# An mLSTM cell with a dropless mixture of experts: keys and queries transposed in fp32 from zero-padded rows, row scaling on GpSimd, clears and weight loads moved

## The chip, the core and the metric

The kernel runs on one core of one Trainium2 chip. The metric is the device time of one execution in microseconds, from the core's first to its last instruction; the number given for a kernel is the median of its timed executions. Engine names in the profile: PE is TensorE (matmul), PEld its weight loads, DVE VectorE, ACT ScalarE, POOL GpSimd, SP SyncE. A `q` after a name (SPq, POOLq) is that engine's sequencer or DMA queue.

## The reference

Two stages. First an mLSTM cell over a sequence, with batch 4, 8 heads, 768 positions and head width 40. It is written as a recurrence:

```python
for t in range(S):
    m_new  = max(f_gate[t] + m, i_gate[t])
    f_stab = exp(f_gate[t] + m - m_new);  i_stab = exp(i_gate[t] - m_new);  m = m_new
    C = f_stab * C + i_stab * outer(v[t], k[t])        # 40 x 40 for each batch and head
    n = f_stab * n + i_stab * k[t]
    y[t] = sigmoid(o_gate[t]) * (C @ q[t]) / max(abs(n . q[t]), 1)
```

Then the rows y (3072 rows of 8 heads x 40 = 320 columns) go through a mixture of 8 experts: `logits = x @ w_gate`, each row goes to the expert with the largest logit, `relu(x @ w1[e]) @ w2[e]` with 1024 hidden columns, times the softmax weight of the chosen expert.

## The kernel before

The recurrence is computed in chunks of 128 positions: 24 steps, 6 chunks for each of 4 batches. Each step s is a pipeline of small functions, run for different s in one pass of the loop. Inside a chunk there is a masked product of queries and keys (`scores`, `attend`); the state from earlier chunks is `C` (`states`). Heads go in pairs (PR = 4 pairs), because two heads of 40 fit on 128 partitions.

```python
DP = 64; DQ = 2 * D; D1 = D + 1                       # D = 40
NKQ = 3
kqb = [consts.tile([128, 2, H, DP], BF16) for i in range(NKQ)]     # bf16 k and q, heads padded to 64
v1  = [consts.tile([128, H, D1], F32) for i in range(NV)]

def first_consts():
    make_identity(nc, ident[:]);  nc.vector.tensor_copy(ident_b[:], ident[:])
    nc.vector.memset(zeros_s[:], 0.0)
    for t in kqb: nc.vector.memset(t[:, :, :, D:], 0.0)
    for t in v1:  nc.vector.memset(t[:, :, D:], 1.0)
    nc.vector.memset(zrow[:], 0.0)
    nc.vector.memset(w1_all[:64, DB - 1], 0.0)        # L91: 64 x 4096 words

def gates():                                          # scans over the sequence, exp, transposes to G_T, m_T
    nc.vector.tensor_tensor_scan(F_sb[:], f_sb[:], zeros_s[:], 0.0, op0=ALU.add, op1=ALU.add)   # L200
    ...

def load(s):                                          # k, q, v, o of one chunk, 160 KB each, on SP
    ...
def casts(s):                                         # L226, L227
    nc.gpsimd.tensor_copy(d["kqb"][:, 0, :, :D], d["k"][:])
    nc.gpsimd.tensor_copy(d["kqb"][:, 1, :, :D], d["q"][:])

def transposes(s):
    for i in range(2):
        for j in range(PR):                           # 8 bf16 transposes, L249
            nc.tensor.transpose(tkq[:, i, j, :], <two heads of kqb>, ident_b[:])
    nc.scalar.copy(d["kqT"][:], tkq[:])               # L253
    if s % NB > 0:
        for j in range(PR):                           # 4 fp32 transposes of q, L257
            nc.tensor.transpose(tq[:, j, :], <two heads of q>, ident[:])
        nc.scalar.copy(d["qT"][:], tq[:])             # L261

def scores(s):                                        # L269, L270; masked to dA (DVE, L274),
    ...                                               # and dB (ACT L276, then POOL affine_select L277)
def states(s):                                        # L289: hp = qT . C;  L297: dC += k . vA;  L303: C = dC * bdm
    ...
def attend(s):                                        # L309: hp += dA or dB . vAb
    ...
def rows(s):
    nc.vector.scalar_tensor_tensor(x3d, in0=th, scalar=1.0, in1=hp[:, :, :D], op0=ALU.add, op1=ALU.mult)   # L321
    <den = max(|2 n.q|, m_T): two operations, L323, L324>
    nc.vector.reciprocal(den[:], den[:])
    nc.vector.tensor_tensor(x3d, x3d, den[:].unsqueeze(2).to_broadcast([128, H, D]), op=ALU.mult)          # L326

def xtrans(s):                                        # three fp32 transposes of x (L333), copied by ACT (L335)
    ...
# logits (L351), choose (L361 to L373), gate, rank (L398), place (L409, L411): the router, for two steps at a time
def keep_rows(t): ...                                 # ACT L416: x_all[:, t] = x * gate weight, bf16
def send(t):      ...                                 # POOL L423: scatter of the rows to x_sorted, by slots
def clear(e):                                         # ACT's DMA queue, L429: zeros to the rows of expert e in x_sorted
    nc.scalar.dma_start(xs[e * NS : e * NS + CAP, :]..., zrow[:])
def weights(e0, n):                                   # POOL's DMA queue, fp32 to bf16: L170 (w1, three parts), L171 (w2)
    ...

for i in range(5): load(i)
for s in range(-3, NT + 3):
    do(load, s + 6 if s >= -1 else -1)
    do(scores, s + 1); do(transposes, s + 2); do(casts, s + 3)
    if s == -3: masks()
    if s == -2: gates(); router()
    do(values, s + 2)                                 # L235: vA = v * G (DVE); L237: vAb = bf16 of vA (POOL)
    if -1 <= s < 3: clear(2 * s + 2); clear(2 * s + 3)
    if not odd and P >= 0: gate(P)
    do(states, s); do(xtrans, s - 1)
    do(ogate, s + 2)                                  # L242: th = tanh(o / 2) (ACT)
    do(attend, s)
    if odd and s >= 3: logits((s - 3) // 2, s)
    if not odd and P >= 0: rank(P, s)
    do(keep_rows, s - 4); do(rows, s)
    if odd and s >= 3: choose((s - 3) // 2)
    if not odd and P >= 0: place(P)
    do(send, s - 5)
    if s == 20: weights(0, 3)                         # w1 and w2 of the first three experts
```

(The tail of the loop, where the last rows are sent, is left out.) After the loop the experts follow: `receive` loads each expert's rows from x_sorted (L538), `turn` transposes them (L569), `layer1` (L578) and `layer2` (L591) multiply, and the results are scattered to the output (L597). A tile of a pool that is full is given out again only when its last reader is done, and PE, ACT, DVE and POOL each take their instructions in the order of the program.

Of the kernel before, what the change touches and what calls it, by code (L numbers as in the profile page):

```python
# [8 lines left out]
F32 = mybir.dt.float32  # L9
BF16 = mybir.dt.bfloat16  # L10
# [4 lines left out]
ALU = mybir.AluOpType  # L15
# [4 lines left out]
def kernel(  # L20
# [13 lines left out]
    nc = tc.nc  # L34
    B, H, S, D = q.shape
    BH = B * H
# [6 lines left out]
    NT = N // 128  # L43
    PR = H // 2
    DP = 64
    DQ = 2 * D
    D1 = D + 1
    LG = H * D1
    RW = Dm + 2
# [22 lines left out]
    ident_b = consts.tile([128, 128], BF16)  # L72
    cmask = consts.tile([128, 128], F32)
    bdm = consts.tile([DQ, PR, 2, D1], F32)
    zeros_s = consts.tile([BH, S], F32)
    NKQ = 3
    kqb = [consts.tile([128, 2, H, DP], BF16, name=f"kqb{i}") for i in range(NKQ)]
    v1 = [consts.tile([128, H, D1], F32, name=f"v1_{i}") for i in range(NV)]
    zrow = consts.tile([128, NJ * RW], BF16)

    def first_consts():
        make_identity(nc, ident[:])
        nc.vector.tensor_copy(ident_b[:], ident[:])
        nc.vector.memset(zeros_s[:], 0.0)

        for t in kqb:
            nc.vector.memset(t[:, :, :, D:], 0.0)
        for t in v1:
            nc.vector.memset(t[:, :, D:], 1.0)
        nc.vector.memset(zrow[:], 0.0)  # L90
        nc.vector.memset(w1_all[:64, DB - 1], 0.0)  # L91

    def masks():

        nc.gpsimd.memset(cmask[:], 1.0)
        nc.gpsimd.affine_select(
            cmask[:], cmask[:], compare_op=ALU.is_ge, fill=0.0,
            base=0, pattern=[[1, 128]], channel_multiplier=-1,
        )

        nc.gpsimd.memset(bdm[:], 1.0)
        nc.gpsimd.affine_select(
            bdm[:], bdm[:], compare_op=ALU.is_ge, fill=0.0,
            base=0, pattern=[[0, PR], [-D, 2], [0, D1]], channel_multiplier=1,
        )
        nc.gpsimd.affine_select(
            bdm[:], bdm[:], compare_op=ALU.is_ge, fill=0.0,
            base=D - 1, pattern=[[0, PR], [D, 2], [0, D1]], channel_multiplier=-1,
        )


# [52 lines left out]
    slots = rte.tile([128, NT], I32)  # L164
    tot = rte.tile([128, E], F32)

    def weights(e0, n):
        e = slice(e0, e0 + n)
        for db, (d0, dsz) in enumerate(dch):
            nc.gpsimd.dma_start(w1_all[128 - dsz :, db, e, :], moe_w1[e, d0 : d0 + dsz, :].rearrange("e p f -> p e f"))  # L170
        nc.gpsimd.dma_start(  # L171
            w2_all[:, e].rearrange("p e a d -> p (e a) d"), moe_w2[e].rearrange("e (a p) d -> p (e a) d", p=128),
        )

    def apart(ins, group):
        ins = getattr(ins, "ins", ins)
# [8 lines left out]

    one_order = ExitStack()
    one_order.enter_context(tc.manual_schedule())
    with tc.tile_pool(name="gates", bufs=1) as gate_pool, \
         tc.tile_pool(name="ld", bufs=6) as ld, \
         tc.tile_pool(name="prep", bufs=3) as prep, \  # L190
         tc.tile_pool(name="chk", bufs=2) as chk, \
         tc.tile_pool(name="ps1", bufs=1, space=PSUM) as ps1, \
         tc.tile_pool(name="ps2", bufs=2, space=PSUM) as ps2:
        st = {}
        f_sb = gate_pool.tile([BH, S], F32)
        i_sb = gate_pool.tile([BH, S], F32)

        def gates():
            F_sb = gate_pool.tile([BH, S], F32)
            nc.vector.tensor_tensor_scan(F_sb[:], f_sb[:], zeros_s[:], 0.0, op0=ALU.add, op1=ALU.add)  # L200
            g_sb = gate_pool.tile([BH, S], F32)
            nc.vector.tensor_sub(g_sb[:], i_sb[:], F_sb[:])
            M_sb = gate_pool.tile([BH, S], F32)
            nc.vector.tensor_tensor_scan(M_sb[:], g_sb[:], g_sb[:], -1e30, op0=ALU.max, op1=ALU.max)
            negc = gate_pool.tile([BH, 1], F32)
            nc.vector.tensor_scalar_mul(negc[:], M_sb[:, S - 1 : S], -1.0)
            for src, e_sb, dst, mul in ((g_sb, F_sb, G_T, 1.0), (M_sb, f_sb, m_T, 2.0)):
                nc.scalar.activation(e_sb[:], src[:], AF.Exp, bias=negc[:], scale=1.0)
                tpg = ps1.tile([128, NB, BH], F32, name="tpg", tag="xt")
                for c in range(NB):  # L210
                    nc.tensor.transpose(tpg[:, c, :], e_sb[:, c * 128 : (c + 1) * 128], ident[:BH, :BH])
                nc.vector.tensor_scalar_mul(
                    dst[:].rearrange("p b c h -> p c b h"), tpg[:].rearrange("p c (b h) -> p c b h", b=B), mul,
                )

        def load(s):
            b, c = s // NB, s % NB
            d = st[s] = {}
            for n, src in (("k", k), ("q", q), ("v", v), ("o", o_gate)):
                d[n] = v1[s % NV] if n == "v" else ld.tile([128, H, D], F32, name=n + "_sb")  # L220
                nc.sync.dma_start(d[n][:, :, :D], src[b, :, c * 128 : (c + 1) * 128, :].rearrange("h p d -> p h d"))

        def casts(s):
            d = st[s]
            d["kqb"] = kqb[s % NKQ]
            nc.gpsimd.tensor_copy(d["kqb"][:, 0, :, :D], d["k"][:])  # L226
            nc.gpsimd.tensor_copy(d["kqb"][:, 1, :, :D], d["q"][:])  # L227

        def values(s):

# [12 lines left out]

        def transposes(s):
            d = st[s]
            tkq = ps1.tile([128, 2, PR, 128], BF16, name="tkq")
            for i in range(2):
                for j in range(PR):
                    nc.tensor.transpose(  # L249
                        tkq[:, i, j, :], d["kqb"][:, i, 2 * j : 2 * j + 2, :].rearrange("p h d -> p (h d)"), ident_b[:],  # L250
                    )
            d["kqT"] = prep.tile([128, 2, PR, 128], BF16, name="kqT")
            nc.scalar.copy(d["kqT"][:], tkq[:])  # L253
            if s % NB > 0:
                tq = ps1.tile([DQ, PR, 128], F32, name="tq")
                for j in range(PR):
                    nc.tensor.transpose(  # L257
                        tq[:, j, :], d["q"][:, 2 * j : 2 * j + 2, :].rearrange("p h d -> p (h d)"), ident[:],
                    )
                d["qT"] = prep.tile([DQ, PR, 128], F32, name="qT")  # L260
                nc.scalar.copy(d["qT"][:], tq[:])  # L261

        def scores(s):
            d = st[s]
            kqT = d["kqT"]
            sA = ps1.tile([128, PR, 128], F32, name="sA")
            sB = ps1.tile([128, PR, 128], F32, name="sB")
            for j in range(PR):
                nc.tensor.matmul(sA[:, j, :], lhsT=kqT[0:D, 0, j, :], rhs=kqT[0:D, 1, j, :], start=True, stop=True)  # L269
                nc.tensor.matmul(  # L270
                    sB[:, j, :], lhsT=kqT[64 : 64 + D, 0, j, :], rhs=kqT[64 : 64 + D, 1, j, :], start=True, stop=True,
                )
            d["dA"] = chk.tile([128, PR, 128], BF16, name="dA")
            nc.vector.tensor_tensor(d["dA"][:], sA[:], cmask[:, None, :].to_broadcast([128, PR, 128]), op=ALU.mult)  # L274
            d["dB"] = chk.tile([128, PR, 128], BF16, name="dB")
            nc.scalar.copy(d["dB"][:], sB[:])  # L276
            nc.gpsimd.affine_select(  # L277
                d["dB"][:], d["dB"][:], compare_op=ALU.is_ge, fill=0.0,
                base=0, pattern=[[0, PR], [1, 128]], channel_multiplier=-1,
            )  # L280

        def states(s):
# [10 lines left out]
            if c + 1 < NB:  # L293
                if c == 0:
                    st["dC"] = ps1.tile([DQ, PR, 2, D1], F32, name="dC")
                for j in range(PR):
                    nc.tensor.matmul(  # L297
                        st["dC"][:, j], lhsT=d["k"][:, 2 * j : 2 * j + 2, :].rearrange("p h d -> p (h d)"),
                        rhs=d["vA"][:, 2 * j : 2 * j + 2, :],
                        start=(c == 0 and j == 0), stop=True, skip_group_check=True,  # L300
                    )
# [12 lines left out]
        def rows(s):  # L314
# [8 lines left out]
            nc.vector.scalar_tensor_tensor(den[:], in0=hp[:, :, D], scalar=-2.0, in1=m_T[:, b, c, :], op0=ALU.mult, op1=ALU.max)  # L323
            nc.vector.scalar_tensor_tensor(den[:], in0=hp[:, :, D], scalar=2.0, in1=den[:], op0=ALU.mult, op1=ALU.max)  # L324
            nc.vector.reciprocal(den[:], den[:])
            nc.vector.tensor_tensor(x3d, x3d, den[:].unsqueeze(2).to_broadcast([128, H, D]), op=ALU.mult)  # L326

        def xtrans(s):

# [101 lines left out]
        def do(f, i, *a):  # L431
            if 0 <= i < NT:
                f(i, *a)
# [5 lines left out]
            nc.scalar.dma_start(wg_sb[128 - dsz :, db, :], moe_w_gate[d0 : d0 + dsz, :])  # L439
        first_consts()  # L440
        for i in range(5):
            load(i)
        for s in range(-3, NT + 3):
            tail = s >= NT
            P, odd = (s - 4) // 2, s % 2
            do(load, s + 6 if s >= -1 else -1)
            do(scores, s + 1)
            do(transposes, s + 2)
            do(casts, s + 3)
            if s == -3:  # L450
                masks()
            if s == -2:
                gates()
                router()
            do(values, s + 2)
            if -1 <= s < 3:
                clear(2 * s + 2)
                clear(2 * s + 3)
            if not odd and P >= 0:
                gate(P)  # L460
            do(states, s)
            do(xtrans, s - 1)
            do(ogate, s + 2)
            do(attend, s)
# [19 lines left out]
                send(s - 3)  # L484
            late_consts(s + 1)
            if s == 20:
                weights(0, 3)

    xg = [x_all[:, e * NJ : (e + 1) * NJ, :] for e in range(E)]
    sm_pool = ctx.enter_context(tc.tile_pool(name="moe_sm", bufs=1))  # L490
# [204 lines left out]
```

## Time and profile before

| | |
|---|---|
| median of 3 timed executions | 250.78 us (249.94 to 251.2) |
| span of the profiled execution | 254.2 us |
| PE busy | 196.4 us, 77% |
| DVE busy | 144.5 us, 57% |
| POOL busy | 134.8 us, 53% |
| ACT busy | 121.1 us, 48% |
| mean granted TensorE clock | 0.877 |
| moved by DMA | 46.46 MB, mean 183 GB/s |

Groups of instructions that the change touches, from the page and the list of groups:

| line, engine, operation | count | busy us | mean ns |
|---|---|---|---|
| L249 PE bf16 transposes of k and q | 192 | 18.8 | 254 |
| L257 PE fp32 transposes of q | 80 | 15.7 | 332 |
| L253 ACT copy of both, 128x1024 bf16 | 24 | 24.4 | 1016 |
| L261 ACT copy of q, 80x512 fp32 | 20 | 11.8 | 588 |
| L226, L227 POOL casts of k and q | 24 each | 17.8, 13.4 | 742, 558 |
| L326 DVE scaling of the rows | 24 | 21.9 | 914 |
| L91 DVE clear of a part of w1 | 1 | 3.5 | 3472 |
| L297 PE, dC from k and vA | 160 | 17.2 | 258 |

How to read the profile: each row of digits has 40 equal slices of the span, and a digit is the busy share in tenths. PEclk is the clock that was granted to TensorE, in tenths of full speed. A row of the timeline gives the start, the duration, the engine and line, what is written from what, the shapes, and in square brackets how long the engine had been idle before and what ended this idle time. Matmuls are pipelined, so their durations overlap; the distance from start to start says what one costs.

### The profile page before, as it was taken

How to read it: one execution, taken by the hardware profiler on the slowest of the kernel's cores; microseconds unless marked ns; L12 is line 12 of the kernel's file. 1: busy time of each engine (PE TensorE's matmuls, PEld its weight loads, DVE VectorE, ACT ScalarE, POOL GpSimd, SP SyncE). 2: the span in 40 equal slices, each digit the busy share in tenths (PEclk: the TensorE clock that was granted, in tenths of full speed). 3: DMA queues.
4: the chain of work that ended last, by engine and by line, in shares of the span. 5: the costliest groups of instructions: out<-in, count | busy, mean ns of one | idle time of the engine just before them, and what ended most of it. 6: DMA issues, size and time to landing. Idle time of an engine off the chain costs nothing. (4 is left out here: it accounts for less than half of the span.)

```text
span 254.2 us, 5437 instructions
## 1 busy us (share of the span) xinstructions
PE 196.4 (77%) x1909; PEld 162.2 (64%) x1909; DVE 144.5 (57%) x439; ACT 121.1 (48%) x277; POOL 134.8 (53%) x214
## 2 busy tenths in 40 slices
PE   0178599869997888879996600499999999999991
PEld 0157499769996787879886500255666666667770
DVE  6946445893659789889785510258345433443550
ACT  2163565773567768668863310034334433444440
POOL 3966456555447577577597328216285443235331
PEclk9999659985589999998997555579999999999999
DMA  8999999995599298990079996999999999314910
GB/s 131 174 179 209 218 228 186 183 175 115 100 200 187 54 165 155 173 166 30 16 117 209 204 197 111 291 247 205 258 219 248 294 416 418 148 59 166 408 50 3
DMA packets 121644, 46.46 MB, mean 183 GB/s; under 512 B 102345, under 2 KB 114764, under 8 KB 121616
## 3 DMA queue, kind: packets, MB, share of 16 engines
q1 hardware_dynamic: 106272, 27.52, 52.1%
q0 software_dynamic: 13728, 16.40, 32.1%
q10 hardware_dynamic: 1616, 2.19, 2.7%
q8 instruction: 15, 0.25, 0.4%
q14 instruction: 13, 0.11, 0.1%
HBM read 39.38 MB, written 9.53 MB: 192 GB/s over the span
## 5 line engine op out<-in xcount | busy, mean ns | idle before, releaser
L583 DVE TENSOR_SCALAR h_sb<-hp 128x384 bf16<-128x384 f32 (+1 forms) x56 | 24.7, 443 | 43.8 <-PE hp L578 26.5
L585 ACT ACTIVATE h_sb<-hp 128x384 bf16<-128x384 f32 (+1 forms) x56 | 22.4, 400 | 38.9 <-PE hp L578 38.5
L597 POOL DMA_INDIRECT out_dram<-zo,s_idx x24 | 24.0, 999 | 31.4 <-ACT zo L596 18.4
L578 PE MATMUL hp<-xgT,w_all 128*128 128x384 bf16 x192 | 34.9, 339 | 0.8 <-issue 0.5
L423 POOL DMA_INDIRECT x_sorted<-x_all,slots x24 | 24.0, 1000 | 13.9 <-ACT x_all L416 5.7
L578 PEld LDWEIGHTS <-w_all 128*128 128x128 bf16 x192 | 19.4, 101 | 14.7 <-issue 3.8
L591 PEld LDWEIGHTS <-h_sb 128*128 128x128 bf16 x240 | 22.9, 98 | 8.1
L277 POOL TENSOR_SCALAR_AFFINE_SELECT dB<-dB 128x512 bf16<-128x512 bf16 x24 | 16.0, 667 | 22.3 <-ACT dB L276 22.2
L253 ACT COPY kqT<-tkq 128x1024 bf16<-128x1024 bf16 x24 | 24.4, 1016 | 6.8 <-PE tkq L249 6.7
L591 PE MATMUL zp<-w_all,h_sb 128*128 128x320 bf16 x192 | 27.4, 299 | 0.0
L249 PE MATMUL tkq<-ident_b,kqb 128*128 128x128 bf16 x192 | 18.8, 254 | 10.3 <-POOL kqb L226 9.8
L596 ACT COPY zo<-zp 128x320 f32<-128x320 f32 x30 | 12.8, 426 | 28.1 <-PE zp L591 28.1
L289 PE MATMUL hp<-C_sb,qT 80*128 80x82 f32 x160 | 23.7, 298 | 1.1 <-DVE C_sb L303 1.1
L289 PEld LDWEIGHTS hp<-C_sb,qT 80*128 80x128 f32 x160 | 22.7, 219 | 1.4 <-ACT xT L335 1.2
L326 DVE TENSOR_TENSOR x_sb<-x_sb,den 128x320 f32<-128x320 f32 x24 | 21.9, 914 | 0.8
L249 PEld LDWEIGHTS <-kqb 128*128 128x128 bf16 x192 | 13.6, 114 | 13.7 <-POOL kqb L226 9.8
L237 POOL CAST vAb<-vA 128x328 bf16<-128x328 f32 x24 | 11.6, 485 | 20.1 <-DVE vA L235 20.1
L351 PE MATMUL hp<-wg_sb,xT 128*128 128x8 f32 x144 | 21.3, 281 | 0.1
L321 DVE SCALAR_TENSOR_TENSOR x_sb<-th,hp 128x320 f32<-128x320 f32 x24 | 11.6, 482 | 16.3 <-PE hp L351 15.2
L569 PE MATMUL tp<-ident_b,x_all 128*128 128x128 bf16 x72 | 7.1, 229 | 17.5 <-DMA x_all<-x_sorted 15.2
L351 PEld LDWEIGHTS hp<-wg_sb,xT 128*128 128x128 f32 x144 | 20.4, 224 | 0.2 <-ACT gex L381 0.2
L335 ACT COPY xT<-xt 128x384 f32<-128x384 f32 x24 | 11.5, 478 | 19.0 <-PE xt L333 15.5
(129 smaller groups left out, 419.1 us busy)
## 6 DMA issues: line engine op xcount, KB each, us to landing
wx<-w_all SPq DMA_DIRECT2D x6, 768.0 KB, 6.5
k_sb<-in_k_dram SPq DMA_DIRECT2D x24, 160.0 KB, 3.9
q_sb<-in_q_dram SPq DMA_DIRECT2D x24, 160.0 KB, 4.2
v<-in_v_dram SPq DMA_DIRECT2D x24, 160.0 KB, 4.1
o_sb<-in_o_gate_dram SPq DMA_DIRECT2D x24, 160.0 KB, 4.1
wx<-w_all SPq DMA_DIRECT2D x6, 640.0 KB, 6.9
w_all<-in_moe_w_dram POOLq DMA_DIRECT2D x5, 640.0 KB, 13.6
w_all<-in_moe_w_dram POOLq DMA_DIRECT2D x10, 256.0 KB, 15.5
```

The costliest lines, as they stand in the source:

```text
L249: nc.tensor.transpose(tkq[:, i, j, :], d["kqb"][:, i, 2 * j : 2 * j + 2, :].rearrange("p h d -> p (h d)"), ident_b[:],)
L253: nc.scalar.copy(d["kqT"][:], tkq[:])
L277: nc.gpsimd.affine_select(d["dB"][:], d["dB"][:], compare_op=ALU.is_ge, fill=0.0, base=0, pattern=[[0, PR], [1, 128]], channel_multiplier=-1,)
L289: nc.tensor.matmul(hp[:, 2 * j * D1 : (2 * j + 2) * D1], lhsT=d["qT"][:, j, :], rhs=st["C"][:, j].rearrange("p h d -> p (h d)"), start=(j ...
L326: nc.vector.tensor_tensor(x3d, x3d, den[:].unsqueeze(2).to_broadcast([128, H, D]), op=ALU.mult)
L351: nc.tensor.matmul(lg[:, i * E : (i + 1) * E], lhsT=st[2 * P + i]["xT"][:, db * 128 : (db + 1) * 128], rhs=wg_sb[:, db, :], start=(fresh a ...
L423: apart(nc.gpsimd.indirect_dma_start(out=xs[:, :], out_offset=bass.IndirectOffsetOnAxis(ap=slots[:, t : t + 1], axis=0), in_=x_all[:, t, : ...
L578: nc.tensor.matmul(hp[:, :cols], lhsT=g["w"][0][:, db, fb * 128 : (fb + 1) * 128], rhs=g["xT"][:, db, :cols], start=(db == 0), stop=(db == ...
L583: nc.vector.tensor_relu(g["h"][:, fb, :cols], hp[:, :cols])
L585: nc.scalar.activation(g["h"][:, fb, :cols], hp[:, :cols], AF.Relu)
L591: nc.tensor.matmul(zp[:], lhsT=g["h"][:, fb, j * 128 : (j + 1) * 128], rhs=g["w"][1][:, fb, :], start=(fb == 0), stop=(fb == FB - 1),)
L597: ins = nc.gpsimd.indirect_dma_start(out=out[:, :], out_offset=bass.IndirectOffsetOnAxis(ap=g["si"](j), axis=0), in_=zo[:], in_offset=None ...
```

## The change

Four things are changed in the first stage; the experts are left as they are.

- **Keys and queries.** The fp32 tiles of k and q have heads padded to 64 columns with zeros, kept in rings of six. They are transposed directly in fp32, and the cast to bf16 is made by ACT in the copy out of PSUM. The casts on GpSimd and the bf16 transposes go. A pair of heads takes 104 rows instead of 80, so the state tiles get 104 partitions.
- **Row scaling.** The multiplication of x by the reciprocal of the denominator moves from VectorE to GpSimd.
- **Clears.** The clear of the part of w1 is made in four pieces at s = 0 to 3; zrow is cleared on GpSimd; the clears of x_sorted move from s = -1 to 2 to s = 0 to 3; the gates use w2's memory as scratch. The load of a step comes after its `states`.
- **Weight loads.** What went out at s = 20 in one go goes out over s = 20, 21 and 22.

```diff
-    DQ = 2 * D
+    DQ = DP + D
...
-        nc.vector.memset(zeros_s[:], 0.0)
-        for t in kqb:
-            nc.vector.memset(t[:, :, :, D:], 0.0)
-        for t in v1:
-            nc.vector.memset(t[:, :, D:], 1.0)
-        nc.vector.memset(zrow[:], 0.0)
-        nc.vector.memset(w1_all[:64, DB - 1], 0.0)
+        nc.vector.memset(zeros_s, 0.0)
+        nc.gpsimd.memset(zrow[:], 0.0)
+    def pads(i):
+        for t in (kp[i], qp[i]):
+            nc.vector.memset(t[:, :, D:], 0.0)
+        nc.vector.memset(v1[i][:, :, D:], 1.0)
...
-        def casts(s):
-            d = st[s]
-            d["kqb"] = kqb[s % NKQ]
-            nc.gpsimd.tensor_copy(d["kqb"][:, 0, :, :D], d["k"][:])
-            nc.gpsimd.tensor_copy(d["kqb"][:, 1, :, :D], d["q"][:])
+        def two(t, j):
+            return t[:, 2 * j : 2 * j + 2, :].rearrange("p h d -> p (h d)")[:, :DQ]
...
-            tkq = ps1.tile([128, 2, PR, 128], BF16, name="tkq")
-            for i in range(2):
+            for n in ("k", "q"):
+                tp = ps1.tile([DQ, PR, 128], F32, name="t" + n)
                 for j in range(PR):
-                    nc.tensor.transpose(tkq[:, i, j, :], <two heads of kqb>, ident_b[:])
-            nc.scalar.copy(d["kqT"][:], tkq[:])
+                    nc.tensor.transpose(tp[:, j, :], two(d[n], j), ident[:])
+                d[n + "b"] = prep.tile([DQ, PR, 128], BF16, name=n + "b")
+                nc.scalar.copy(d[n + "b"][:], tp[:])
             if s % NB > 0:
-                tq = ps1.tile([DQ, PR, 128], F32, name="tq")
-                for j in range(PR):
-                    nc.tensor.transpose(tq[:, j, :], <two heads of q>, ident[:])
                 d["qT"] = prep.tile([DQ, PR, 128], F32, name="qT")
-                nc.scalar.copy(d["qT"][:], tq[:])
+                nc.scalar.copy(d["qT"][:], tp[:])
...
-            nc.vector.tensor_tensor(x3d, x3d, den[:].unsqueeze(2).to_broadcast([128, H, D]), op=ALU.mult)
+            nc.gpsimd.tensor_tensor(x3d, x3d, den[:].unsqueeze(2).to_broadcast([128, H, D]), op=ALU.mult)
...
         for s in range(-3, NT + 3):
-            do(load, s + 6 if s >= -1 else -1)
             do(scores, s + 1)
             do(transposes, s + 2)
-            do(casts, s + 3)
...
-            if -1 <= s < 3:
-                clear(2 * s + 2)
-                clear(2 * s + 3)
+            if 0 <= s < E // 2:
+                nc.vector.memset(w1_all[:64, DB - 1, 2 * s : 2 * s + 2, :], 0.0)
+                clear(2 * s)
+                clear(2 * s + 1)
...
             do(states, s)
+            do(load, s + 6 if s >= -1 else -1)
...
             if s == 20:
-                weights(0, 3)
+                weights_in(0, 3, (0, 1))
+            if s == 21:
+                weights_in(0, 3, (2,))
+                weights_out(0, 2)
+            if s == 22:
+                weights_out(2, 1)
```

## The prediction

> **What bounds the kernel now.** I read the 40-slice rows first, to cut the span into stages, then the timeline of each stage, because the share of busy time mixes stages and the page's chain of waits holds nothing here but the last scatter (0.3% of the span).
>
> ```profile
> PE   0178599869997888879996600499999999999991
> DVE  6946445893659789889785510258345433443550
> PEclk9999659985589999998997555579999999999999
> DMA  8999999995599298990079996999999999314910
> ```
>
> One slice is 254.2 / 40 = 6.36 us. Slices 0 to 2 are the start (PE nearly idle), 3 to 21 the 24 attention steps, 22 to 25 a hole in PE, and 26 to 39 the experts, where PE is full at full clock. The change touches only the first three. In the attention steps PE is full, but not always; the timeline of two steps at full clock shows what interrupts it:
>
> ```profile
> 95.48 0.95 DVE L326 TENSOR_TENSOR x_sb<-x_sb,den 128x320 f32<-128x320 f32 x1
> 98.18 0.21 PE L269 MATMUL sA<-kqT 40*128 40x128 bf16 x1 [0.51 <-DVE dA L274]
> 99.95 1.68 DVE L326 TENSOR_TENSOR x_sb<-x_sb,den 128x320 f32<-128x320 f32 x1
> 100.81 0.45 POOL L226 CAST kqb<-k_sb 128x320 bf16<-128x320 f32 x1
> 101.21 0.72 POOL L227 CAST kqb<-q_sb 128x320 bf16<-128x320 f32 x1
> 101.77 0.52 PE L333 MATMUL xt<-ident,x_sb 128*128 128x128 f32 x3 [0.77 <-DVE sm L409]
> ```
>
> PE waits 0.51 + 0.77 = 1.28 us in this pair of steps, both times behind DVE, and DVE is late because the row scaling L326 takes 0.95 and 1.68 us. In the tail, with no cast beside it, the same instruction took 0.49. The pair runs from scores at 94.27 to scores at 103.74: 9.47 us, of which 8.2 is dense PE. Per step that is 4.74, of which 4.1 is PE.
>
> The start is set by DVE and GpSimd:
>
> ```profile
> 4.44 3.47 DVE L91 MEMSET w_all<- 64x4096 uint32 x1 [0.80 <-DMA f_sb<-in_f_gate_dram]
> 4.56 5.22 POOL L226 CAST kqb<-k_sb 128x320 bf16<-128x320 f32 x1 [3.20 <-DMA k_sb<-in_k_dram]
> 7.84 1.68 DVE L200 TENSOR_TENSOR_SCAN F_sb<-f_sb,zeros_s 32x768 f32<-32x768 f32 x1
> 27.58 0.47 ACT L242 ACTIVATE th<-o_sb 128x320 f32<-128x320 f32 x1 [4.17 <-DMA x_sorted<-zrow]
> ```
>
> The gate scan sits behind a 3.47 us clear, and the first cast, usually 0.45 us, takes 5.22. The last line is a second hold-up: ACT stood 4.17 us before issuing a clear of x_sorted, and PE then ran at half clock from about 27 to 39 us.
>
> The hole:
>
> ```profile
> 152.05 0.95 POOL L423 DMA_INDIRECT x_sorted<-x_all,slots  x1 [3.48 <-DMA w_all<-in_moe_w_dram]
> 161.56 0.82 PE L569 MATMUL tp<-ident_b,x_all 128*128 128x128 bf16 x6 [15.22 <-DMA x_all<-x_sorted]
> ```
>
> The last row scatter waits for the 1920 KB w2 load that went out at 130.0, and the experts wait for the rows.
>
> **What the Trainium skill says.** "SBUF — State Buffer", section "Who interferes with whom": a VectorE instruction with two SBUF inputs and a GpSimd instruction that reads SBUF exclude each other for a whole instruction, and who comes first decides. The trace agrees: L326 has 0.49 us at the shortest, 0.86 in the median, 1.94 at most. "GPSIMD Engine Reference", section 3.1: a two-input fp32 tensor_tensor of 2048 elements takes 4497 ns, 2.2 ns an element; the trace has no such GpSimd instruction. "TensorE: Matmul & The Clock Gate", "LDWEIGHTS": a load costs its columns, not its rows. The trace agrees: 174 ns for the 80 columns of k_sb against 219 for 128 columns of qT. The same page, Part 1, has the clock fall to half after too little PE work and come back after some 3.4 us of it; this trace agrees on the fall, but from 55.5 to 72.5 us the clock stayed at half with PE full, so I don't count on the return.
>
> **The change, part by part.**
>
> *Start.* The 3.47 us clear leaves the front of DVE and zrow's 0.46 goes to GpSimd. Eighteen small pads take the place of nine: twelve of 192 words at about 0.21 us (kqb's: 0.63 for three) and six at 0.03, some 2.7 us. zeros_s ended at 2.4, so the scan can begin at about 5.1 instead of 7.84: 2.7 us earlier. The casts of k and q on GpSimd are gone, so the first transposes no longer wait until 9.83. Loads don't wait for the pads, which touch other columns. The gates are then the longest path to the first scores.
>
> *Clears.* Two per step at s = 0 to 3 instead of -1 to 2, and the load of the step now follows them in program order. In the built program each clear still waits for an earlier load's semaphore, at s = 1 q and o of load 5. The loads run at DMA pace (4 x 160 KB issued every 3.7 us), and o of load 5 was issued at 22.9 and would land at about 27, while s = 1 could come at 24 to 26. So ACT will still stand here and part of the 2.7 us is eaten. The four pieces of the w1 clear, 3.47 / 4 = 0.87 us each, come to DVE in these steps. ACT's tanh marks a step: the one of s = 3 began at 40.26; I put it at 36.5 to 37, **3.5 us gained**.
>
> *Steps, PE.* Out: 8 bf16 transposes, 0.46 us from start to start (94.60 to 95.06). In: 4 fp32 transposes of k, like those of q (0.43, 95.06 to 95.49). dC's stationary k grows from 80 to 104 columns: from 82 ns a record to perhaps 95, eight records, +0.1. Dense PE stays at 4.1 to 4.2 us a step.
>
> *Steps, DVE.* L326 goes: 0.95 and 1.68 in the pair, 1.3 a step out of about 4.5. DVE has then about 3.2 us of work in a step of 4.2.
>
> *Steps, GpSimd.* Out: two casts, 742 + 558 = 1.3 us. In: the scaling, estimated from the skill's page at 320 x 2.2 = 0.70 plus some 0.15, 0.85 us. It must be done before the transposes of x in the next step: PE reaches those 2.8 us after the end of the logits (0.33 scores, 0.87 transposes, 1.6 states); DVE's four small operations end 1.05 us after it and the scaling at about 2.1. It fits with 0.7 to spare.
>
> *Steps, ACT.* One copy of 1016 ns becomes two like L276 (577): +0.1 us of about 3.4 a step, below PE.
>
> So a step falls from 4.74 to about **4.2**, bound by PE. From s = 3 to s = 20 the kernel before took 85.2 us (40.26 to 125.44); 17 x 4.74 = 80.6, and the other 4.6 are stretches at half clock. After: 17 x 4.2 = 71.4, plus 3.5 for half clock, which I expect less often with PE denser but don't trust: 75, **10 us gained**.
>
> *Hole.* The 3.84 MB of weights took from 128 to 151.3, at about 200 GB/s with the DMA engines full; spread over three steps they still follow each other without a gap and end some 23 us after the first. But the last scatter now follows the w2 load of two experts and no longer the last one, and can be queued before the weights are all in. I give it **2 us**.
>
> *Experts.* 161.5 to the end: untouched, 0.
>
> Sum: 3.5 + 10 + 2 = 15.5 us from the profiled 254.2. The timed executions are 3.4 us shorter than the profiled one, and I don't know which stage had those; I take off 2 from the gain. 250.8 - 13.5 = **237.3 us**.
>
> **The rivals.**
>
> *The loads become the bound.* 640 KB a step at the 175 to 180 GB/s seen between 4 and 20 us is 3.65 us; DMA is at 9 tenths until 110 us. For: the margin to 4.2 is small, and the clears add 1.9 MB. Against: SP issued load 12 at 52 to 56 us, two to three steps before its use. If it binds, 2 to 4 us of the gain go: 240.
>
> *The scaling on GpSimd is slow.* If it takes 1.6 us or more, or stands behind the mask of dB and the scatter (1.0 us), the transposes of x wait as before, for POOL instead of DVE. For: no such instruction was measured. Against: GpSimd falls to about 3.2 us a step. Then 244 or so.
>
> *The clock.* If half clock takes as much or more of the steps than before, nothing of the 4.6 comes back: 241 or, with 10 us more of it, 245.
>
> *The hole swallows it.* If weights reach the end of the steps later relative to the rows, the 2 us are not won: 239. The weights start at the same step, so what is gained before s = 20 can't be lost here.
>
> **Range and chances.** Good cases stack up to 230 (no half clock in the steps); two of the rivals together give 245 to 246. "Faster by over 2%" means under 245.8. Nothing that I found makes a stage longer by more than 1 us, so slower needs a mechanism that I missed, mostly GpSimd.
>
> **What would show it.** Scan at 5 to 5.5 us; tanh of s = 3 near 36.5; steps of 4.2 us, PE without waits for DVE in them; no L326 on DVE, a GpSimd tensor_tensor of 0.8 to 1.0 us; the time from the first weights to PE's first expert transposes 31 to 32 us instead of 33.7; experts 92 to 93 us. I am wrong if PE's transposes of x wait for POOL, if SP's loads are what PE waits for, or if the clock row has more than three slices under 7 before the hole.

## The result and the profile after

The changed kernel takes **238.64 us** (median of 4 executions, 234.84 to 243.16) against 250.6 (249.94 to 251.2) for the kernel before, timed beside it: a ratio of 0.940, 95% interval 0.934 to 0.947. Ratios, here and below, compare only the executions within 1.5% of their kernel's fastest (here 235.6 us on average against 250.6, 15 us apart), while the medians take in all of them. The prediction was 237.3 us, in a range of 230 to 246.

The profiled executions differ by more than that: 254.2 us before, 234.2 after, a difference of 20.0. As timed, these two took 255.96 and 236.42 us: the one before was longer than the four that give the median of its kernel, and the one after was shorter than the median of its four. So the stages below add up to 20, and only 12 of them show between the medians.

The 40-slice rows of the changed kernel (one slice is 5.86 us):

```profile
PE   2289789999999999999562007999999999999990
DVE  7657845588668766976343002783452354334540
PEclk9999995999999999999955555999999999999998
DMA  7999999999898999943999999999999999117900
```

PE is now at nine tenths without a break from slice 6 to slice 18, which the row of before never was. DVE, busy for 86% of six steps at full clock before, is busy for 75% of six steps now. The clock row has a single five before the hole. The hole is slices 19 to 23, about as wide as before.

The same stages in both profiles, cut at ACT's tanh of s = 3, the tanh of s = 20 and PE's first expert transposes:

| stage | before, us | after, us | gain |
|---|---|---|---|
| start to tanh of s = 3 | 40.26 | 36.65 | 3.6 |
| s = 3 to s = 20 | 85.2 | 67.8 | 17.4 |
| s = 20 to first expert transposes | 36.1 | 37.0 | -0.9 |
| experts | 92.6 | 92.75 | -0.1 |

Two steps at full clock, from the timelines of POOL and PE. The third column is the engine, and a bracket would stand at the end of a PE row that waited:

```profile
74.10 0.72 POOL L324 TENSOR_TENSOR x_sb<-x_sb,den 128x320 f32<-128x320 f32 x1 [0.57 <-DVE sm L407]
74.97 0.49 PE L331 MATMUL xt<-ident,x_sb 128*128 128x128 f32 x3
78.19 0.72 POOL L324 TENSOR_TENSOR x_sb<-x_sb,den 128x320 f32<-128x320 f32 x1 [0.97 <-DVE lmin L359]
79.76 0.49 PE L331 MATMUL xt<-ident,x_sb 128*128 128x128 f32 x3
```

The scaling on GpSimd takes 0.72 us here and ends at 74.82 and 78.91; PE takes up x at 74.97 and 79.76 without a wait, with 0.15 and 0.85 us to spare. From 35 to 100 us no row of PE has a bracket at all.

The start:

```profile
4.93 1.73 DVE L209 TENSOR_TENSOR_SCAN w_all<-w_all 32x768 f32<-32x768 f32 x1
26.70 0.48 ACT L333 COPY xT<-xt 128x384 f32<-128x384 f32 x1 [3.74 <-DMA o_sb<-in_o_gate_dram]
32.02 0.48 ACT L333 COPY xT<-xt 128x384 f32<-128x384 f32 x1 [2.54 <-DMA v<-in_v_dram]
36.65 0.47 ACT L247 ACTIVATE th<-o_sb 128x320 f32<-128x320 f32 x1
```

The scan begins 2.9 us earlier than before. ACT stands 3.74 and 2.54 us, released by a load that its copy of xT doesn't use; just ahead of each stand ACT had to issue two clears of x_sorted.

The hole:

```profile
128.16 0.97 POOL L421 DMA_INDIRECT x_sorted<-x_all,slots  x1 [0.26 <-issue]
134.89 4.98 SPq L545 DMA_DIRECT2D x_all<-x_sorted  x8
141.45 0.82 PE L576 MATMUL tp<-ident_b,x_all 128*128 128x128 bf16 x6 [15.80 <-DMA x_all<-x_sorted]
```

and SP's reading back of the rows in the kernel before:

```profile
154.93 5.05 SPq L538 DMA_DIRECT2D x_all<-x_sorted  x8
```

The last row scatter no longer waits for a weight load: it goes out 20.4 us after the first weights (107.72), where it was 24.2 before. But SP can read the rows back only at 134.89, 6.7 us after the last scatter, where it was 2.9. From the first weights to PE's transposes it is 33.73 us, exactly as before.

### The profile page after: what moved, and what is told of

Its sections match the earlier page's. It is cut to its first block, busy times and chain, and to the rows that moved or that the text cites. A ratio compares the mean times of both kernels' runs of the same rounds, so it can differ in the third digit from the quotient of the medians.

```text
span 234.2 us, 5321 instructions
## 1 busy us (share of the span) xinstructions
PE 190.8 (81%) x1829; PEld 158.2 (68%) x1829; DVE 125.0 (53%) x426; ACT 121.5 (52%) x301; POOL 125.2 (53%) x192
## 5 line engine op out<-in xcount | busy, mean ns | idle before, releaser
L590 DVE TENSOR_SCALAR h_sb<-hp 128x384 bf16<-128x384 f32 (+1 forms) x56 | 24.6, 443 | 44.0 <-PE hp L585 26.7
L324 POOL TENSOR_TENSOR x_sb<-x_sb,den 128x320 f32<-128x320 f32 x24 | 17.4, 724 | 25.9 <-DVE lmin L359 13.6
L421 POOL DMA_INDIRECT x_sorted<-x_all,slots x24 | 25.8, 1074 | 5.1 <-issue 3.6
L319 DVE SCALAR_TENSOR_TENSOR x_sb<-th,hp 128x320 f32<-128x320 f32 x24 | 11.5, 481 | 22.8 <-PE hp L349 19.3
L287 PE MATMUL hp<-C_sb,qT 104*128 104x82 f32 x160 | 21.4, 279 | 0.6 <-DVE C_sb L301 0.6
L254 PE MATMUL tk<-ident,kp 128*104 128x128 f32 x96 | 17.4, 310 | 4.3 <-POOL bdm L102 4.3
L287 PEld LDWEIGHTS hp<-C_sb,qT 104*128 104x128 f32 x160 | 20.3, 199 | 0.9 <-ACT xT L333 0.7
L349 PE MATMUL hp<-wg_sb,xT 128*128 128x8 f32 x144 | 20.1, 273 | 0.0
L275 POOL TENSOR_SCALAR_AFFINE_SELECT dB<-dB 128x512 bf16<-128x512 bf16 x24 | 17.4, 723 | 4.3 <-ACT dB L274 4.0
L295 PE MATMUL dC<-vA,kp 128*104 128x82 f32 x160 | 19.2, 267 | 0.0
L576 PEld LDWEIGHTS <-x_all 128*128 128x128 bf16 x72 | 5.2, 102 | 20.0 <-DMA x_all<-x_sorted 15.9
L274 ACT CAST dB<-sB 128x512 bf16<-128x512 f32 x24 | 14.0, 583 | 7.7 <-PE sB L268 7.7
```

Of the source, the lines that this page charges most:

```text
L254: nc.tensor.transpose(tp[:, j, :], two(d[n], j), ident[:])
L275: nc.gpsimd.affine_select(d["dB"][:], d["dB"][:], compare_op=ALU.is_ge, fill=0.0, base=0, pattern=[[0, PR], [1, 128]], channel_multiplier=-1,)
L287: nc.tensor.matmul(hp[:, 2 * j * D1 : (2 * j + 2) * D1], lhsT=d["qT"][:, j, :], rhs=st["C"][:, j].rearrange("p h d -> p (h d)"), start=(j ...
L295: nc.tensor.matmul(st["dC"][:, j], lhsT=two(d["k"], j), rhs=d["vA"][:, 2 * j : 2 * j + 2, :], start=(c == 0 and j == 0), stop=True, skip_g ...
L324: nc.gpsimd.tensor_tensor(x3d, x3d, den[:].unsqueeze(2).to_broadcast([128, H, D]), op=ALU.mult)
L349: nc.tensor.matmul(lg[:, i * E : (i + 1) * E], lhsT=st[2 * P + i]["xT"][:, db * 128 : (db + 1) * 128], rhs=wg_sb[:, db, :], start=(fresh a ...
```

## The experiments

### The scaling alone, and the rest without it

Two kernels split the gain of the steps. The first is the changed kernel with one word put back:

```diff
-            nc.gpsimd.tensor_tensor(x3d, x3d, den[:].unsqueeze(2).to_broadcast([128, H, D]), op=ALU.mult)
+            nc.vector.tensor_tensor(x3d, x3d, den[:].unsqueeze(2).to_broadcast([128, H, D]), op=ALU.mult)
```

> The changed kernel with the row scaling back on VectorE; everything else as changed, so GpSimd has no casts of k and q. Theory A (VectorE was late because the casts excluded it, and taking the casts away is what counts): the scaling takes 0.5 to 0.8 us on VectorE instead of 0.95 to 1.7, VectorE has about 3.8 us of work in a step, PE stays the bound, a pair of steps at full clock takes 7.9 to 8.2 us and the time is within 2 us of the changed kernel. Theory B (the move itself is what counts): PE again waits for VectorE before scores and before the transposes of x, a pair takes 9 us or more, and the time is 8 to 12 us above the changed kernel.

Measured: 246.82 us, against 253.71 for the kernel before on the same chip, ratio 0.977 (0.972 to 0.982). The timelines of DVE and PE in two of its steps:

```profile
97.14 0.94 DVE L324 TENSOR_TENSOR x_sb<-x_sb,den 128x320 f32<-128x320 f32 x1
99.94 0.21 PE L267 MATMUL sA<-qb,kb 40*128 40x128 bf16 x1 [0.42 <-DVE dA L272]
101.61 1.30 DVE L324 TENSOR_TENSOR x_sb<-x_sb,den 128x320 f32<-128x320 f32 x1
103.05 0.52 PE L331 MATMUL xt<-ident,x_sb 128*128 128x128 f32 x3 [0.85 <-DVE sm L407]
```

The casts of k and q are gone from GpSimd here, and the scaling on DVE is still slow: 828 ns on average, 914 before. With it come back the same two waits of PE. So taking the casts away does little for this instruction; it has to leave DVE. While it ran long, GpSimd was at the mask of dB (97.11 to 97.74) or at a scatter and the next mask (100.88 to 102.55). The Trainium skill, "SBUF — State Buffer", section "Who interferes with whom", has such a VectorE instruction shut out by any GpSimd instruction that reads SBUF, not by casts alone. The times agree, and in the kernel before the scaling at 131.61 us took 0.94 us beside the mask (131.49 to 132.19) with the casts of k and q over; but no run took the mask or the scatters away.

The second is the kernel before with the same word changed the other way, so that GpSimd has the scaling and the casts as well:

> The kernel before with the row scaling on GpSimd, nothing else. Theory A (casts and scaling must not both be on GpSimd): GpSimd has select 0.65, casts 1.1 to 1.3, vAb 0.46, scaling 0.72 and scatter 1.15, some 4.2 us a step, next to PE's 4.1; PE waits for GpSimd before the transposes of k and q or of x; a pair of steps takes 8.6 to 9.2 us, and the time is 3 to 6 us below the kernel before. Theory B (moving the scaling is the whole gain of the steps): a pair takes 8.0 to 8.3 us and the time is 9 to 12 us below the kernel before.

Measured: 245.47 us on the same chip, ratio 0.990 (0.977 to 1.003), too wide to call. Its steps are clear:

```profile
86.13 0.80 PE L249 MATMUL tkq<-ident_b,kqb 128*128 128x128 bf16 x8 [0.69 <-POOL kqb L226]
95.01 0.80 PE L249 MATMUL tkq<-ident_b,kqb 128*128 128x128 bf16 x8 [1.08 <-POOL kqb L226]
```

PE now waits for the casts, 0.69 and 1.08 us, behind a GpSimd that had no idle time just before. Six successive steps at full clock, and the whole stage, took:

| kernel | six steps, us | per step | s = 3 to s = 20, us |
|---|---|---|---|
| before | 28.44 | 4.74 | 85.2 |
| after, scaling on DVE | 26.99 | 4.50 | 80.8 |
| before, scaling on GpSimd | 26.06 | 4.34 | 72.7 |
| after | 23.80 | 3.97 | 67.8 |

The move alone is worth 2.4 us in six steps, everything else without it 1.45, both together 4.6. Over the whole stage the two kernels with the scaling on DVE took 4.6 and 4.3 us more than 17 such steps, and had stretches at half clock; the two with it on GpSimd took 0.3 us more and nothing. These are single profiles, and no run shows why the stretches went. The casts have to go so that GpSimd has room for the scaling, and the scaling has to go so that DVE keeps up.

### What the split of the weight loads is worth

The changed kernel with the loads of three experts in one go at s = 20:

```diff
-                weights_in(0, 3, (0, 1))
-            if s == 21:
-                weights_in(0, 3, (2,))
-                weights_out(0, 2)
-            if s == 22:
-                weights_out(2, 1)
+                weights(0, 3)
```

> The changed kernel with the weights of three experts issued at s = 20 in one go, as before. Theory A (the bytes of the weights ahead of the rows in one queue bind the hole, not how they are split): from the first weight load to the first transposes of the experts 33 to 34.5 us, as in both kernels (33.7), and the same time within 1.5 us. Theory B (the split wins something that another new wait eats): 35.5 us or more, and 2 us slower.

Measured: 240.15 us (236.0 to 242.78), which doesn't part from the changed kernel. First weights to first expert transposes: 33.96 us against 33.73. The wait at the last scatter is back:

```profile
132.68 0.96 POOL L421 DMA_INDIRECT x_sorted<-x_all,slots  x1 [1.95 <-DMA w_all<-in_moe_w_dram]
```

So the split takes away the visible wait and wins nothing: with it, the wait is in the landing of the rows instead. The nine scatters of rows issued from 105 us on in the changed kernel took 9.0 us to land, in the median.

The counter-test leaves the same place in the program but takes bytes away from ahead of the rows. Only expert 0 is loaded at s = 20, and the others after the last scatter:

```diff
             if s == 20:
-                weights_in(0, 3, (0, 1))
+                weights(0, 1)
...
-    weights(3, 1)
-    weights(4, 1)
+    weights(1, 1)
+    weights(2, 1)
...
-        if 5 + i < E:
-            weights(5 + i, 1)
+        if 3 + i < E:
+            weights(3 + i, 1)
```

> The changed kernel with only the weights of expert 0 (1.28 MB) at s = 20; those of experts 1 and 2 follow the last scatter, and the others come three experts ahead instead of five. Theory A (bytes bind): the weights are through 7 to 8 us after their issue, long before the last slots (18 us after it); the last scatter lands 4 us after the last slots, and the experts' first transposes come 26 to 29 us after the first weight load instead of 33.7: 5 to 7 us faster than the changed kernel. Theory B (the hole is the chain of router, scatter, receive, whatever is loaded): 32 to 34 us, and no gain. What could spoil A: the weights of experts 1 and 2 come late, and PE waits for them at experts 1 to 3.

```profile
136.81 0.82 PE L571 MATMUL tp<-ident_b,x_all 128*128 128x128 bf16 x6 [11.34 <-DMA x_all<-x_sorted]
193.44 0.65 PE L580 MATMUL hp<-xgT,w_all 128*128 128x384 bf16 x3 [0.64 <-issue]
194.91 0.65 PE L580 MATMUL hp<-xgT,w_all 128*128 128x384 bf16 x3 [0.82 <-issue]
```

The hole shrinks to 29.1 us (107.70 to 136.81), as expected: SP reads the rows back 3.2 us after the last scatter instead of 6.7. With fewer bytes ahead of them the rows land sooner: this shows the cause. But the span, 234.4, is no shorter than the 234.2 of the changed kernel: the experts take 97.6 us instead of 92.75. PE stops near 193 us in the first layer of expert 6, whose weights went out only at 173.69 (the trace names nothing that these waits end with), and SP's copies of weights for the overflow blocks, which need all of w_all, begin at 191.3 instead of 179.8. In this profile the gain of the hole was given back at the end. Timed: 236.15 us (232.52 to 236.23), which overlaps the changed kernel's range; the kernel with three experts in one go took 240.15 on this chip, so part of the gain may have stayed.

### The clears that ACT issued

The changed kernel with the clears of x_sorted on GpSimd's queue:

```diff
-            nc.scalar.dma_start(xs[e * NS : e * NS + CAP, :].rearrange("(p j) d -> p (j d)", j=NJ), zrow[:])
+            nc.gpsimd.dma_start(xs[e * NS : e * NS + CAP, :].rearrange("(p j) d -> p (j d)", j=NJ), zrow[:])
```

> The changed kernel with the clears of x_sorted issued by GpSimd in place of ACT; nothing else differs. Theory A: ACT's waits of 3.74 and 2.54 us in the first steps are its queue standing at a clear until an earlier load has landed. With the clears on GpSimd's queue ACT goes on, the tanh of s = 3 comes at 31 to 34 us in place of 36.65, the slice at half clock near 38 us goes, and the kernel gains 3 to 5 us: 233 to 236. Theory B: the loads themselves set the pace there (640 KB a step at 175 to 180 GB/s), so ACT or PE then waits for the loads in place of the clears, tanh of s = 3 comes at 35.5 to 37 and the time stays within 1 us. Theory C: GpSimd now stands at the clears in ACT's place, and its row scaling and mask of dB come late: PE waits for POOL in the first steps, and the kernel is 1 to 3 us slower.

Measured: **233.52 us** (232.71 to 234.01), ratio to before 0.934 (0.928 to 0.940). The rows of PE and of its clock, from the page:

```profile
PE   1389999999999999996560019989999999999980
PEclk9999999999999999999555555999999999999998
```

and the tanh of s = 3, from the timeline of ACT:

```profile
31.71 0.47 ACT L247 ACTIVATE th<-o_sb 128x320 f32<-128x320 f32 x1
```

Theory A holds in each point. From 16 us to the end of the steps PE has no wait, the half clock near 38 us is gone, and the tanh comes 4.9 us earlier than in the changed kernel. Of these the profile's end shows 2.1 (span 232.1), because the hole grew from 33.73 to 35.3 us and the experts from 92.75 to 93.8. Between the medians it is 5.1 us, but they come from different chips, and the intervals of the two ratios overlap. Two pairs of kernels below differ by the same edit on one chip each, by 3.7 and by 1.4 us.

It doesn't settle the question of the spread. The four executions of this kernel lie within 1.3 us, those of the changed kernel within 8.3, and within 3.8 when it ran again. But of the kernels below one with the clears on ACT, on this same chip, lies within 1.7, and two with them on GpSimd, on another, within 5.5 and 5.7. The changed kernel again:

> The changed kernel itself, beside the other two on the same chip, so that they can be compared with it and not only with the kernel before. 235 to 241 us as before; the spread between its executions should again come from stretches at half clock before 45 us.

Measured: 238.40 us (236.92 to 240.69), ratio 0.943 (0.933 to 0.953). Its profiled execution has the tanh of s = 3 at 39.31 instead of 36.65, with stands of ACT of 4.84 and 3.50 us, and a span of 236.3: the start lost 2.7 us, the steps won 1.8 of it back, the rest of the span lost 1.3, and the span grew by 2.1. So how long ACT stands at the clears differs between two executions of one program. My guess about half clock failed in that profile, where the clock dipped only to 0.7 in one slice.

### Larger pieces, and both edits together

The hole's gain should be kept if the later weights came sooner. Expert 0 at s = 20, then two experts in each transfer (the diff is against the run with one expert ahead):

```diff
-    weights(1, 1)
-    weights(2, 1)
+    weights(1, 2)
+    weights(3, 2)
...
-        if 3 + i < E:
-            weights(3 + i, 1)
+        if 5 + i < E:
+            weights(5 + i, 1)
```

> The changed kernel with the weights of expert 0 alone issued at s = 20; after the last row scatter those of experts 1 and 2 in one go, then 3 and 4 in one go, then one expert in each group as in the changed kernel. Theory A: the version with one expert ahead reached PE's first expert transposes 4.6 us sooner and gave it all back because its last weights were issued one group later each and in small pieces, so that the copies for the overflow blocks, which need all of w_all, came at 191 us in place of 180; with fewer and larger pieces the copies come by 185, the hole is 29 to 30 us, the experts take 93 to 95, and the time falls by 2 to 4 us against the changed kernel. Theory B: the DMA engines are full from the last scatter on, so that the bytes not moved in the hole are missing at the end whatever the order: hole 29 to 30, experts 96 to 98, time within 1 us of the changed kernel.

Measured: 242.23 us, ratio 0.969 (0.963 to 0.976); both theories missed. The hole is 30.3 us as expected, but the experts take 102.2. From the timelines of POOL and PE:

```profile
151.43 0.92 POOL L171 DMA_DIRECT2D w_all<-in_moe_w_dram  x1 [10.39 <-DMA w_all<-in_moe_w_dram]
175.73 3.52 PE L580 MATMUL hp<-xgT,w_all 128*128 128x384 bf16 x12 [6.98 <-ACT h_sb L587]
```

and from its list of transfers issued between 124 and 170 us (queue, count, KB of each if told, median us from issue to landing):

```profile
w_all<-in_moe_w_dram POOLq DMA_DIRECT2D x2, 1280.0 KB, 26.6
out_dram<-zo,s_idx POOLq DMA_INDIRECT x3, 17.7
```

The large pieces take 26.6 us to land. GpSimd, which also sends out the results, stands 10.4 us before it can issue the next weight load, and the scatters of the results then land 17.7 us after issue. PE stops for 7 us. The page's chain of waits gives weights 9% of the span and these scatters 8%. This version was worse, but two things in it are not separated: the pieces are larger, and five experts' weights are queued ahead of the first scatter of results, where the changed kernel and the one with one expert ahead queue three after the last rows.

The same with the clears on GpSimd:

> The two edits together: clears on GpSimd's queue and one expert ahead in larger pieces. If both theories A hold, the gains add, 5 to 8 us under the changed kernel: 230 to 234. If the clears bring nothing and the bytes bind at the end, within 1 us of it.

Measured: 238.53 us, ratio 0.955 (0.950 to 0.961), 3.7 us less than without the clears on the same chip, but PE again stops, for 9.3 us. The gain of the clears repeats; that of the larger pieces isn't there.

So I went back to the small pieces, with the clears on GpSimd:

> The changed kernel with the clears on GpSimd's queue and only expert 0's weights issued at s = 20, the others one by one after the last row scatter as in the run with one expert ahead. Theory A (both parts keep what they showed alone): first weights at 103, PE's first expert transposes 29 us later, experts 97.6 us, span about 230 and time 231 to 233, hardly better than the clears alone, because the copies for the overflow blocks come late. Theory B: the part that was late at the end is caught up, experts 93 to 94 and the time 227 to 229.

Measured: **228.99 us** (227.72 to 233.21), ratio to before 0.907 (0.899 to 0.916). This beats both kernels: the changed one, run on the same chip, took 238.40. Its profiled execution was its slowest. The row of PE on its page has eights in the steps,

```profile
PE   2289998999988899999965018989999999999990
```

and its timeline says what for, in one of several such steps:

```profile
68.01 0.62 PE L254 MATMUL tq<-ident,qp 128*104 128x128 f32 x4 [1.08 <-DMA qp<-in_q_dram]
```

PE's listed waits in these steps add up to 4.1 us, 2.7 of them for k and q and the rest for ACT. There s = 3 to s = 20 took 72.9 us, against 67.9 with the clears alone. Up to s = 20 the two are the same program, so this comes from the chip or the execution, not from the edit: the three kernels that had the clears on GpSimd on other chips took 67.9 to 68.0. The hole was 30.2 us and the experts 93.4: theory B's figure, though the weights were as late as with one expert ahead. Why they cost 97.6 there and 93.4 here is not settled. The other three executions were 3.1 to 5.5 us shorter; that they had fewer of these waits is likely, but they have no profile.

Last, one expert's weights more in the gap in which the DMA engines were idle (the diff is against the kernel just described):

```diff
             if s == 20:
                 weights(0, 1)
+            if s == 21:
+                weights(1, 1)
```

(experts 2 to 4 follow after the last scatter, the others as in the changed kernel)

> The changed kernel with the clears on GpSimd's queue, expert 0's weights at s = 20, expert 1's at s = 21, and those of 2, 3 and 4 one by one after the last row scatter, the others as in the changed kernel. With one expert ahead the DMA engines were nearly idle while the last rows were sent; theory A says that 1.3 MB more fit into that gap and land before the last scatter, so the hole stays at 29 to 31 us and the experts, no longer short of weights, take 93 to 95: span 226 to 228, time 228 to 230. Theory B: any weights issued after s = 20 stand ahead of the last rows or hold GpSimd at a semaphore: hole 32 to 34, time 231 to 234, no better than the clears alone.

Measured: 238.23 us (235.78 to 241.47), no better than the changed kernel. The hole was 32.5 us, theory B's figure, and PE waited for q in the steps here too. From the timelines of POOL and PE:

```profile
112.41 1.66 POOL L167 DMA_DIRECT2D w_all<-in_moe_w_dram  x3
114.04 0.96 POOL L171 DMA_DIRECT2D w_all<-in_moe_w_dram  x1
115.57 0.77 POOL L324 TENSOR_TENSOR x_sb<-x_sb,den 128x320 f32<-128x320 f32 x1
116.39 0.90 PE L331 MATMUL xt<-ident,x_sb 128*128 128x128 f32 x3 [2.09 <-POOL tick L420]
```

The bytes did fit: SP read the rows back 3.4 us after the last scatter (129.54 to 132.91), about as soon as with one expert ahead. But the last scatter came 22.8 us after the first weights, against 20.7 with the clears on GpSimd and one expert ahead. GpSimd was issuing expert 1's weights for 2.6 us before it came to the mask and the row scaling of that step, and PE waited 2.09 us for it, a wait that the profile with one expert ahead doesn't show at this place. So of theory B the second half fits, with GpSimd held by the issuing itself and not by a semaphore. No run tests this alone.

### What the earlier scan is worth

The clear of w1 put back in front as one operation, with the clears of x_sorted where the changed kernel has them, and then with them on GpSimd:

```diff
         nc.gpsimd.memset(zrow[:], 0.0)
+        nc.vector.memset(w1_all[:64, DB - 1], 0.0)
...
-                nc.vector.memset(w1_all[:64, DB - 1, 2 * s : 2 * s + 2, :], 0.0)
```

> The changed kernel with the clear of w1's unused rows put back as one operation of some 3.5 us at the front of DVE, and taken out of the steps 0 to 3. The scan begins near 8.4 us in place of 4.93. Theory A: at s = 1 ACT stands at a clear of x_sorted until a load lands, and loads are issued at DMA pace whatever DVE does, so the tanh of s = 3 stays within 1 us of the 36.65 of the changed kernel (36 to 38) and the time within 1 us of it: the earlier scan was eaten by that stand. Theory B: the start's 3 us come from the earlier scan; tanh of s = 3 at 39 to 40.5 and the time 3 us longer, 241 to 242.

> The same with the clears of x_sorted on GpSimd's queue, where ACT has no stand that could eat the delay. Theory A: here the 3.5 us at the front count in full: tanh of s = 3 at 34.5 to 35.5 in place of 31.71, time 2.5 to 4 us above the run with the clears on GpSimd alone (236 to 237.5). Theory B: the loads' pace sets this too, and the tanh of s = 3 stays at 31.5 to 33, the time within 1 us of it.

The first scores came 4.3 us later in both (20.20 and 20.19 us, from 15.92 and 15.91). With ACT at the clears, 2.7 of these were left at the tanh of s = 3 (39.36) against the first profile of the changed kernel, and none against the second (39.31), and the time was 236.8 us (235.25 to 240.24), no longer than the changed kernel's; neither theory gave both numbers. With the clears on GpSimd nearly all of it arrived, 4.1 us: 35.83 against 31.71, and 235.41 us (234.75 to 236.23) against 233.52; the rest came back in the hole and the experts. So a part of the earlier scan, or all of it, is eaten by ACT's stands, and the clear's new place is worth some 2 us once these are gone (by medians of different chips, and by the spans, 234.0 and 232.1). For the changed kernel itself its worth is not settled; the start differs by as much between its executions.

## Why the prediction was right, step by step

- **Start: 3.5 us predicted, 3.6 measured.** The scan came at 4.93 for 5.1, and ACT stood where I said, released by o of load 5 at 26.7 (I had 27). The run with the clears on GpSimd shows that the stand is these clears. That the size came out to within 0.1 is luck: the second profile of the changed kernel has the tanh of s = 3 at 39.31, a gain of only 1.0.
- **Steps, the mechanism: right.** PE's waits for DVE are gone, and the two splits show that both halves of it are needed. The GpSimd scaling that I put at 0.85 us measured 0.72, or 2.26 ns an element: the rate of the Trainium skill's "GPSIMD Engine Reference", section 3.1, holds to 3% at this size, and the 0.15 that I added was too much. DVE does 3.0 us of work a step (I had 3.2), GpSimd 2.9 (3.2), ACT 3.4. The 0.7 us to spare were too much: in one of the two steps shown it is 0.15.
- **Steps, the size: 10 us predicted, 17.4 measured.** Two terms were mis-sized. *The step.* Dense PE was right for the pair I read: scores to scores 3.52 and 4.78, a mean of 4.15. But one step in six has no dC and one has no product with the old state; the 24.9 us of six steps become 23.8, 3.97 a step. In the kernel before, where PE waited for DVE, the steps took 4.58 to 4.90 us whatever PE had to do in them, so I didn't see it; in the changed kernel they take 3.09 to 4.79. 17 x 3.97 = 67.5, against my 71.4. *Half clock.* I kept 3.5 us; the clock was at full speed in nearly all of that stage, and only 0.3 us are left for it. So of the 17.4 some 13 are shorter steps, and 4.3 are half clock that went; I expected less of it but counted on 1.1 only, and no run explains it.
- **dC: right in direction, small in effect.** Its eight records went from 0.57 to 0.73 us, start to start: 0.16 where I had 0.1.
- **Hole: 2 us predicted, none measured.** The step that failed is "can be queued before the weights are all in". It was queued earlier, 20.4 us after the first weights and not 24.2, but landed behind the weights' bytes, and the rows were read back 6.7 us later and not 2.9; one expert's bytes instead of three's brought 4.6 us. The rival "the hole swallows it" was this.
- **Experts: 92 to 93 predicted, 92.75.**
- **Profile to median: 2 us taken off, 8 needed.** I compared a span (254.2) with timed medians: as timed, the profiled execution before took 255.96, so it stood 5.2 us above the median of 250.78 and not 3.4. The stages gained 20.0, not 15.5, and the medians differ by 12.0. The two errors, 4.5 and 6, nearly cancel: that the total is within 1.3 us is luck. The executions that are shorter than the profiled one before, and longer than the profiled one after, have no profile.
- **Rivals.** GpSimd was not too slow. The loads did not bind in the changed kernel, but PE waited for q in two kernels that had the clears on GpSimd, both on one chip, and in none of the three on other chips, so that rival is the next limit in some executions.

## What to carry to other kernels

When a queued transfer ahead of the last data is moved, ask which bytes stand before it in the same queue, not only which wait ends last: the wait can vanish and the time stay. Move an instruction to another engine together with what makes room for it there, and check the step in which it has the least to spare. Size a loop over its whole period, since steps with less work are hidden as long as another engine binds, and count once that engine is relieved.

## What the runs showed of the hardware

- In this program an engine that issues a transfer stood for an earlier load: ACT 3.74 us for o, 2.54 for v; GpSimd 10.4 us with 1280 KB transfers ahead. With the clears on GpSimd's queue ACT waited for no load there, and PE for nothing.
- The fp32 product over 128x320 elements (x times den) took 0.72 to 0.73 us on average on GpSimd in the kernels that had it there, and 0.49 to 1.94 on DVE. The price for the neighbours was small: the DVE product of v and the gates rose from 528 to 611 ns, GpSimd's mask from 667 to 723 ns.
- Larger transfers brought nothing here: with the clears on GpSimd, the kernel with 1280 KB pieces took 238.53 us and the one with single experts' pieces 228.99, on different chips, but the first also had more experts' weights queued at once; scatters behind them landed after 17.7 us.
